# Transposing q and k by crossbar DMA instead of on TensorE, in a fused attention and feed-forward kernel

## The chip, the cores and the metric

The kernel runs on one core of one Trainium2 chip. The metric is device time in microseconds (us). Three runs of the kernel before gave a median of 439.14 us (439.12 to 439.34).

Names: PE is TensorE, PEld its weight loads, DVE is VectorE, ACT is ScalarE, POOL is GpSimd, SP is SyncE. SP issues the output stores and, after the change, the transposing DMAs; GpSimd issues the input loads. "L216" is line 216 of the kernel.

## The reference

Eight batches of eight heads, 576 tokens, head size 64, float32 inputs. Attention with a relative bias, then a feed-forward layer:

```python
scores = scale * np.matmul(q, k.transpose(0, 1, 3, 2))     # q, k, v: (8, 8, 576, 64)
scores = scores + bias.transpose(2, 0, 1)[None]            # bias_table[bucket(|i - j|)]
attn = exp(scores - max) / sum                             # softmax
x = np.matmul(attn, v)                                     # -> (4608, 512)
h = x @ w_in                                               # 512 -> 2048
out = np.maximum(0.01 * h, h) @ w_out                      # 2048 -> 512
```

## The kernel before

The kernel works on pairs of heads: 32 pairs, four to a batch. The score matmul needs q and k with the head dimension on the partitions. They are loaded with tokens on the partitions: partition `r` of 96 holds tokens `6r` to `6r+5`. So each pair's q and k are copied into a dense tile (`pr`), transposed on PE into PSUM in six blocks of 96 rows by 128 columns (the profile shows each as a matmul of 96x96), and copied out by VectorE, which also puts the tokens in order.

```python
pr_pool = ctx.enter_context(tc.tile_pool(name="pr", bufs=4))
ps_m_pool = ctx.enter_context(tc.tile_pool(name="ps_m", bufs=3, space=bass.MemoryType.PSUM))
# ... (cut)
def transpose_q(n):
    qs = prs.pop((n, "q"))
    ps = ps_m_pool.tile([P, 8 * P], BF16, name="ps_tq", tag="m")
    for c in range(NC):                                    # NC = 6, RQ = 96
        nc.tensor.transpose(ps[:, c * RQ : (c + 1) * RQ], in_=qs[0:RQ, c, :],
                            identity=ident[0:RQ, 0:RQ])
    qt = qt_pool.tile([P, S], BF16, name="qt")
    nc.vector.tensor_copy(out=qt.rearrange("p (r c) -> p r c", c=NC),
                          in_=ps[:, 0:S].rearrange("p (c r) -> p r c", c=NC))
    qts[n] = qt
# ... transpose_k is alike, and ends with two small copies inside kt
```

The main loop, one iteration per pair, interleaves everything. `moe(1)` emits one piece of feed-forward work: a group of four first-layer matmuls and its activation ("in"), or four second-layer matmuls ("out"). Pieces exist only once enough tokens have been through attention.

```python
for n in range(N + 1):
    # ... loads of later batches (cut)
    pair_rows(n + 1, "q"); pair_rows(n + 1, "k")           # VectorE: dense rows of the next pair
    ps_a, ps_b = qk_mm(n, 0), qk_mm(n, 1)                  # PE: scores; ps_s has two buffers
    exp_band(n, 0, ps_a)                                   # ScalarE: exp; VectorE: bias factor
    moe(1)
    exp_band(n, 1, ps_b)
    av(n - 1, 0)                                           # PE: attention times v; VectorE: divide
    transpose_q(n + 1)
    moe(1)
    ps_a, ps_b = qk_mm(n, 2), qk_mm(n, 3)
    exp_band(n, 2, ps_a)
    moe(1)
    exp_band(n, 3, ps_b)
    av(n - 1, 1)
    transpose_k(n + 1)
    # ... scores 4 and 5, x_transposes(n - 1), five more pieces (cut)
moe_rest()                                                 # what is left of the feed-forward layer
```

In the traces here PE, ScalarE and VectorE run their instructions in the order of the program, so an instruction that waits holds up everything behind it on its engine.

The softmax here doesn't subtract the row's maximum and nothing guards it: scores larger than these inputs give would overflow.

Of the kernel before, what the change touches and what calls it, by code (L numbers as in the profile page):

```python
# [11 lines left out]
BF16 = mybir.dt.bfloat16  # L12
# [25 lines left out]
def kernel(  # L38
# [10 lines left out]
    nc = tc.nc  # L49

    B, H, S, D = q.shape
# [4 lines left out]
    P = 128  # L56
# [12 lines left out]

    per = ctx.enter_context(tc.tile_pool(name="per", bufs=1))  # L70
    qt_pool = ctx.enter_context(tc.tile_pool(name="qt", bufs=2))
    pr_pool = ctx.enter_context(tc.tile_pool(name="pr", bufs=4))
    op_pool = ctx.enter_context(tc.tile_pool(name="op", bufs=2))
    rc_pool = ctx.enter_context(tc.tile_pool(name="rc", bufs=4))
    gt_pool = ctx.enter_context(tc.tile_pool(name="gt", bufs=2))
# [3 lines left out]
    ps_m_pool = ctx.enter_context(tc.tile_pool(name="ps_m", bufs=3, space=bass.MemoryType.PSUM))  # L79

    ident = per.tile([P, P], BF16, name="ident")
# [8 lines left out]
    NBUF = 2  # L90
    RQ = 96
    NC = S // RQ
    qn = [per.tile([P, H, NC, D], BF16, name=f"qn{i}") for i in range(NBUF)]
    kn = [per.tile([P, H, NC, D], BF16, name=f"kn{i}") for i in range(NBUF)]
    vn = [per.tile([P, NJ, H, D + 1], BF16, name=f"vn{i}") for i in range(NBUF)]
    v4 = [per.tile([P, n_pairs, 2, D + 1], BF16, name=f"v4_{i}") for i in range(NBUF)]
    kts_ = [per.tile([P, S + P], BF16, name=f"kt{i}") for i in range(2)]
# [6 lines left out]
    def load_qk(b, h0, h1):  # L104
        i = b % NBUF
        for src, dst in ((q, qn[i]), (k, kn[i])):
            nc.gpsimd.dma_start(
                out=dst[0:RQ, h0:h1, :, :].rearrange("r h c d -> r h (c d)"),
                in_=src[b, h0:h1, :, :].rearrange("h (r c) d -> r h (c d)", c=NC),
            )  # L110

    def load_v(b, h0, h1, by_head):
        i = b % NBUF
        p0, p1 = h0 // 2, h1 // 2
        if by_head:
            for h in range(h0, h1):
                nc.gpsimd.dma_start(
                    out=vn[i][:, :, h, 0:D],
                    in_=v[b, h, 0 : NJ * P, :].rearrange("(c s) d -> s c d", s=P),
                )  # L120
        else:
            for c in range(NJ):
                nc.gpsimd.dma_start(  # L123
                    out=vn[i][:, c, h0:h1, 0:D],
                    in_=v[b, h0:h1, c * P : (c + 1) * P, :].rearrange("h s d -> s h d"),
                )
        for e in range(2):
            nc.gpsimd.dma_start(
                out=v4[i][e * SL : (e + 1) * SL, p0:p1, e, 0:D],
                in_=v[b, h0 + e : h1 : 2, NJ * P : S, :].rearrange("h s d -> s h d"),  # L130
            )
# [6 lines left out]
    for i in range(2):  # L138
# [12 lines left out]
        out=tab.rearrange("p u h -> p (u h)"),  # L151
        in_=bass.AP(tensor=bias_table.tensor, offset=bias_table.offset, ap=[[0, P], [1, NB * H]]),
# [10 lines left out]
    for u, lo, hi in bucket_runs(NB, BAND, S):  # L163
        if lo >= small:
            nc.vector.tensor_copy(
                out=ub[:, :, C0 + lo : C0 + hi + 1],
                in_=e8[:, :, u : u + 1].to_broadcast([P, H, hi - lo + 1]),
# [3 lines left out]
        out=ub[:, :, C0 - BAND + 1 : C0],  # L171
        in_=bass.AP(tensor=row.tensor, offset=row.offset + C0 + BAND - 1,
                    ap=[list(row.ap[0]), [UW, H], [-1, BAND - 1]]),
# [4 lines left out]
    for h0, h1 in ((0, 2), (2, H)):  # L178
        nc.sync.dma_start(
            out=eb[:, h0:h1, :],  # L180
            in_=bass.AP(tensor=urows, offset=h0 * UW + P - 1, ap=[[H * UW - 1, P], [UW, h1 - h0], [1, 3 * P]]),
        )
    for e in range(2):
        nc.sync.dma_start(
            out=eb4[e * SL : (e + 1) * SL, :, :],
            in_=bass.AP(tensor=urows, offset=e * UW + P - 1, ap=[[H * UW - 1, SL], [2 * UW, n_pairs], [1, P + SL]]),
        )

    def load_weights():
        for c in range(n_cc):  # L190
            nc.gpsimd.dma_start(out=w_in_sb[:, c, :], in_=moe_w_in[c * P : (c + 1) * P, :])
        for g in range(n_fc // 4):
            nc.gpsimd.dma_start(
                out=w_out_sb[:, 4 * g : 4 * g + 4, :],
                in_=moe_w_out[g * 512 : (g + 1) * 512, :].rearrange("(f p) e -> p f e", p=P),
            )


    items = [(b, p) for b in range(B) for p in range(n_pairs)]
    qts, kts, ops_ = {}, {}, {}  # L200

    prs = {}

    def pair_rows(n, which):
        src = {"q": qn, "k": kn}[which]
        b, p = items[n]
        t = pr_pool.tile([RQ, NC, 2 * D], BF16, name="pr")
        nc.vector.tensor_copy(out=t.rearrange("r c (e d) -> r c e d", e=2),  # L208
                              in_=src[b % NBUF][0:RQ, 2 * p : 2 * p + 2, :, :].rearrange("r e c d -> r c e d"))
        prs[n, which] = t  # L210

    def transpose_q(n):
        qs = prs.pop((n, "q"))
        ps = ps_m_pool.tile([P, 8 * P], BF16, name="ps_tq", tag="m")
        for c in range(NC):
            nc.tensor.transpose(ps[:, c * RQ : (c + 1) * RQ], in_=qs[0:RQ, c, :],  # L216
                                identity=ident[0:RQ, 0:RQ])
        qt = qt_pool.tile([P, S], BF16, name="qt")
        nc.vector.tensor_copy(out=qt.rearrange("p (r c) -> p r c", c=NC),  # L219
                              in_=ps[:, 0:S].rearrange("p (c r) -> p r c", c=NC))  # L220
        qts[n] = qt

    def transpose_k(n):
        ks = prs.pop((n, "k"))
        ps = ps_m_pool.tile([P, 8 * P], BF16, name="ps_tk", tag="m")
        for c in range(NC):
            nc.tensor.transpose(ps[:, c * RQ : (c + 1) * RQ], in_=ks[0:RQ, c, :],  # L227
                                identity=ident[0:RQ, 0:RQ])
        kt = kts_[n % 2]
        nc.vector.tensor_copy(out=kt[:, 0:S].rearrange("p (r c) -> p r c", c=NC),  # L230
                              in_=ps[:, 0:S].rearrange("p (c r) -> p r c", c=NC))
        for e in range(2):
            r = slice(e * D, (e + 1) * D)
            nc.vector.tensor_copy(out=kt[r, S + e * SL : S + (e + 1) * SL], in_=kt[r, NJ * P : S])
        kts[n] = kt

    def qk_mm(n, u):

        qt, kt = qts[n], kts[n]
        ps = ps_s_pool.tile([P, 2, 512], FP32, name="ps_s")  # L240
        if u < NJ:
            for e in range(2):
                r = slice(e * D, (e + 1) * D)
                nc.tensor.matmul(ps[:, e, :], lhsT=kt[r, u * P : (u + 1) * P], rhs=qt[r, 0:512],  # L244
                                 start=True, stop=True)
        elif u == NJ:
            for c in range(NJ):
                for e in range(2):
                    r = slice(e * D, (e + 1) * D)
                    nc.tensor.matmul(ps[:, e, c * SL : (c + 1) * SL], lhsT=kt[r, c * P : (c + 1) * P],  # L250
                                     rhs=qt[r, 512:S], start=True, stop=True)
        else:
            nc.tensor.matmul(ps[:, 0, :], lhsT=kt[:, S : S + P], rhs=qt[:, 0:512], start=True, stop=True)  # L253
            nc.tensor.matmul(ps[:, 1, 0:SL], lhsT=kt[:, S : S + P], rhs=qt[:, 512:S], start=True, stop=True)
        return ps
# [123 lines left out]
    def finished(n):  # L379
        b, p = items[n]  # L380
        if p == n_pairs - 1:
            while made["ready"] < n_tt and (made["ready"] + 1) * TT <= (b + 1) * S:
                made["ready"] += 1

    pair_rows(0, "q")
    pair_rows(0, "k")
    transpose_q(0)
    transpose_k(0)
    N = len(items)
    for n in range(N + 1):  # L390
        live = n < N
        if live:
            b, p = items[n]
            if n == 0:
                load_qk(1, 0, H)
                load_weights()
                load_v(1, 0, H, False)
            elif p == 1 and 0 < b < B - 1:
                load_qk(b + 1, 0, H)
                load_v(b + 1, 0, H, False)  # L400
            if n + 1 < N:
                pair_rows(n + 1, "q")
                pair_rows(n + 1, "k")
            ps_a, ps_b = qk_mm(n, 0), qk_mm(n, 1)
            exp_band(n, 0, ps_a)
        moe(1)
        if live:
            exp_band(n, 1, ps_b)
        if n > 0:
            av(n - 1, 0)  # L410
        if n + 1 < N:
            transpose_q(n + 1)
        moe(1)
        if live:
# [3 lines that stand above are left out]
        if live:  # L418
            exp_band(n, 3, ps_b)
        if n > 0:  # L420
            av(n - 1, 1)
        if n + 1 < N:
            transpose_k(n + 1)
        moe(1)
        if live:
            ps_a, ps_b = qk_mm(n, 4), qk_mm(n, 5)
            exp_band(n, 4, ps_a)
        moe(1)
        if n > 0:
            x_transposes(n - 1)  # L430
            finished(n - 1)
        moe(1)
        if live:
            exp_band(n, 5, ps_b)
        moe(2)
# [31 lines left out]
```

## Time and profile before

The profile has five stages. The copies into `pr` come once per iteration, so the distance between them in the timeline is the time per pair:

| stage, us | time per pair, us | what sets it |
|---|---|---|
| 0 to 42 | - | first loads and the bias table |
| 42 to 69 | 6.1 to 6.8 | attention alone, VectorE nearly full |
| 69 to 103 | 8.5 | attention and "in" pieces |
| 103 to 364 | 11.08 | attention, "in" and "out" pieces: PE full |
| 364 to 438 | - | feed-forward alone, PE full |

The windows view of the kernel before: each row is a stretch of time, its length, the busy time and (number of) instructions of PE, PEld, DVE, ACT and POOL, then granted clock, DMA share and GB/s.

```profile
45.00:50.00 5.00, 5.00 (x77) 3.56 (x75) 4.30 (x13) 3.67 (x6) 0.57 (x2) 1.00 1.77 184
50.00:55.00 5.00, 3.79 (x62) 2.17 (x58) 4.36 (x12) 3.87 (x6) 1.29 (x2) 1.00 1.70 154
55.00:60.00 5.00, 4.06 (x81) 2.83 (x80) 4.80 (x14) 4.14 (x5) 0.00 (x0) 1.00 0.89 136
60.00:65.00 5.00, 3.86 (x71) 2.52 (x70) 4.75 (x14) 4.63 (x6) 0.63 (x1) 1.00 0.10 7
...
120.00:160.00 40.00, 40.00 (x411) 20.32 (x408) 24.73 (x63) 26.27 (x37) 6.00 (x8) 1.00 0.40 56
```

From 120 us PE is busy all the time, with VectorE at about 60% and ScalarE at about 66% (24.73 and 26.27 of 40 us). And from 45 to 55 us the DMA share is 1.7: packets overlap in time, and their times add up to 1.7 times the span of all 16 DMA engines. By their landing times (when their data has arrived) these are the last of the weight loads; the v loads of the second batch; and the q and k loads of the third batch, issued at 49.7 and 51.2 us.

What the PE transposes cost, in the timeline (start, us, engine, line, operation; "x6" is six instructions merged):

```profile
205.47 0.19 PE L303 MATMUL ps_o<-v_0_106,at_1_113 128*128 128x65 bf16 x1
205.50 0.42 PE L216 MATMUL ps_tq<-ident,pr 96*128 96x96 bf16 x6
205.75 0.60 PE L338 MATMUL pm_2911<-w_out_sb,gt 128*128 128x512 bf16 x2
```

One transpose is 206 ns long (the tile view of `ps_tq`), but they are pipelined: six of them hold up the next matmul by 0.25 us. q and k together take 0.51 us of PE per pair.

### The profile page before, as it was taken

What the parts mean: (1) busy time and instruction counts of PE and PEld (TensorE: products, weight loads), DVE (VectorE), ACT (ScalarE), POOL (GpSimd) and SP (SyncE); (2) the same over time, 40 slices, a digit from 0 to 9 for tenths busy, and PEclk for the clock granted to TensorE, in tenths of its full rate; (3) what the DMA queues carried; (4) which work ended last, traced back from release to release, by engine and by line L of the source; (5) the groups of instructions that cost most, each with busy time, mean ns of one, the idle gap of its engine ahead of it and who ended that gap; (6) DMA issues with size and microseconds to landing.
All of it is one profiled execution on the core that took longest, in us unless ns stands there. A gap on an engine that the chain in (4) does not pass through costs nothing.

```text
span 438.2 us, 9059 instructions
## 1 busy us (share of the span) xinstructions
PE 392.3 (90%) x3872; PEld 202.3 (46%) x3872; DVE 229.1 (52%) x581; ACT 247.1 (56%) x338; POOL 60.8 (14%) x84
## 2 busy tenths in 40 slices
PE   0511888999999999999999999999999999999996
PEld 0201554555555555555555555555555454444442
DVE  7331897666666666666666666666666542010111
ACT  1401787887666666666666666666666653333310
POOL 9522103103100310031003100300000000000000
PEclk9999999999999999999999999999999999999999
DMA  8999948708531853184418350900000000101111
GB/s 108 230 225 214 172 71 53 109 4 54 92 65 28 76 83 76 29 76 73 86 27 76 65 94 26 80 25 25 25 25 25 25 25 25 48 29 44 49 48 73
DMA packets 60216, 30.53 MB, mean 70 GB/s; under 512 B 39312, under 2 KB 54800, under 8 KB 60176
## 3 DMA queue, kind: packets, MB, share of 16 engines
q0 software_dynamic: 52960, 18.36, 37.6%
q1 hardware_dynamic: 7216, 11.60, 7.6%
q8 instruction: 30, 0.49, 0.5%
q14 instruction: 10, 0.08, 0.1%
HBM read 37.81 MB, written 10.49 MB: 110 GB/s over the span
## 4 chain that ended last, share of the span: by engine, by line
PE 79%; DVE 7%; DMA 7%; ACT 5%; issue 2%; SPq 0%; DVEq 0%; ACTq 0%
PE ps_o L301 7%; PE ps_s L244 6%; DMA eb_99<-u_rows 5%; PE ps_s L253 2%; DMA u_rows<-ub 2%; PE ps_o L303 2%; ACT at_110 L264 2%; ACT at_111 L264 2%; PE ps_tx L315 2%; PE ps_tq L216 1%; PE ps_tk L227 1%; PE ps_s L250 1%; DVE at_110 L288 1%; DVE opair L307 1%; ACT gt L329 1%
## 5 line engine op out<-in xcount | busy, mean ns | idle before, releaser
L264 ACT ACTIVATE at_111<-ps_s 128x1024 bf16<-128x1024 f32 x64 | 64.7, 1021 | 38.4 <-PE ps_s L244 38.3
L327 PEld LDWEIGHTS <-w_in_sb 128*128 128x128 bf16 x576 | 49.9, 98 | 72.6 <-issue 21.7
L338 PEld LDWEIGHTS <-gt 128*128 128x128 bf16 x576 | 52.6, 98 | 51.4 <-issue 0.4
L264 ACT ACTIVATE at_110<-ps_s 128x1024 bf16<-128x1024 f32 x64 | 64.3, 1021 | 20.6 <-PE ps_s L244 20.4
L288 DVE TENSOR_TENSOR at_110<-at_110,eb 128x512 bf16<-128x512 bf16 (+1 forms) x64 | 32.3, 506 | 53.0 <-ACT at_110 L264 36.8
L288 DVE TENSOR_TENSOR at_111<-at_111,eb 128x512 bf16<-128x512 bf16 (+1 forms) x64 | 32.3, 506 | 44.1 <-ACT at_111 L264 40.0
L244 PE MATMUL ps_s<-qt,kt_109 64*128 64x512 bf16 x128 | 20.8, 396 | 13.7 <-DVE kt_109 L230 13.1
L301 PEld LDWEIGHTS <-at_110 128*128 128x128 bf16 x640 | 28.3, 100 | 10.0 <-DVE opair L307 3.0
L307 DVE TENSOR_TENSOR opair<-ps_o,rcp 128x320 bf16<-128x320 f32 x64 | 31.5, 492 | 2.2
L301 PEld LDWEIGHTS <-at_111 128*128 128x128 bf16 x640 | 27.2, 98 | 9.9 <-DVE opair L307 3.0
L216 PE MATMUL ps_tq<-ident,pr 96*128 96x96 bf16 x192 | 14.2, 212 | 11.5 <-DVE pr L208 11.5
L219 DVE COPY qt<-ps_tq 128x576 bf16<-128x576 bf16 x32 | 23.9, 748 | 0.4 <-PE ps_tq L216 0.4
L244 PE MATMUL ps_s<-qt,kt_108 64*128 64x512 bf16 x128 | 21.6, 403 | 2.3 <-DVE kt_108 L230 1.2
L303 PE MATMUL ps_o<-v_0_106,at_0_112 128*128 128x65 bf16 x80 | 13.7, 200 | 8.9 <-DVE at_0_112 L288 8.8
L303 PEld LDWEIGHTS <-at_0_112 128*128 128x128 bf16 x160 | 15.9, 99 | 9.2 <-DVE at_0_112 L288 9.2
L306 DVE RECIPROCAL rcp<-ps_o 128x5 f32<-128x5 f32 x64 | 12.2, 191 | 11.4 <-PE ps_o L303 11.4
L244 PEld LDWEIGHTS <-kt_109 64*128 64x128 bf16 x128 | 4.2, 94 | 28.1 <-issue 13.8
L301 PE MATMUL ps_o<-vn_104,at_110 128*128 128x65 bf16 x320 | 15.8, 200 | 0.9 <-DVE opair L307 0.8
L123 POOL DMA_DIRECT2D vn_105<-in_v_dram x16 | 14.1, 888 | 15.5 <-PE ps_o L303 7.6
L301 PE MATMUL ps_o<-vn_104,at_111 128*128 128x65 bf16 x320 | 14.5, 194 | 1.7 <-DVE opair L307 1.7
L216 PEld LDWEIGHTS <-pr 96*128 96x128 bf16 x192 | 10.0, 101 | 12.5 <-DVE pr L208 12.4
L303 PEld LDWEIGHTS <-at_1_113 128*128 128x128 bf16 x160 | 15.6, 97 | 0.2 <-DVE at_1_113 L288 0.2
(867 smaller groups left out, 819.1 us busy)
## 6 DMA issues: line engine op xcount, KB each, us to landing
out_dram<-y SPq DMA_DIRECT2D x36, 256.0 KB, 2.0
qn_101<-in_q_dram POOLq DMA_DIRECT2D x4, 576.0 KB, 6.2
kn_103<-in_k_dram POOLq DMA_DIRECT2D x4, 576.0 KB, 8.3
w_in_sb<-in_moe_w_in_dram POOLq DMA_DIRECT2D x4, 512.0 KB, 18.5
w_out_sb<-in_moe_w_out_dram POOLq DMA_DIRECT2D x4, 512.0 KB, 23.0
vn_105<-in_v_dram POOLq DMA_DIRECT2D x16, 128.0 KB, 5.1
qn_100<-in_q_dram POOLq DMA_DIRECT2D x3, 576.0 KB, 6.0
kn_102<-in_k_dram POOLq DMA_DIRECT2D x3, 576.0 KB, 8.8
```

The costliest lines, as they stand in the source:

```text
L123: nc.gpsimd.dma_start(out=vn[i][:, c, h0:h1, 0:D], in_=v[b, h0:h1, c * P : (c + 1) * P, :].rearrange("h s d -> s h d"),)
L216: nc.tensor.transpose(ps[:, c * RQ : (c + 1) * RQ], in_=qs[0:RQ, c, :], identity=ident[0:RQ, 0:RQ])
L219: nc.vector.tensor_copy(out=qt.rearrange("p (r c) -> p r c", c=NC), in_=ps[:, 0:S].rearrange("p (c r) -> p r c", c=NC))
L244: nc.tensor.matmul(ps[:, e, :], lhsT=kt[r, u * P : (u + 1) * P], rhs=qt[r, 0:512], start=True, stop=True)
L264: nc.scalar.activation(at[:, :, u, 0:512], ps, AF.Exp, scale=scale)
L288: nc.vector.tensor_tensor(out=o, in0=o, in1=m, op=ALU.mult)
L301: nc.tensor.matmul(ps[:, ic, :], lhsT=at[:, o : o + P], rhs=vn[i][:, c, 2 * p + e, :], start=(c == 0), stop=False)
L303: nc.tensor.matmul(ps[:, ic, :], lhsT=at4[:, ic * P : (ic + 1) * P], rhs=v4[i][:, p, e, :], start=False, stop=True)
L306: nc.vector.reciprocal(rcp, ps[:, :, D : D + 1])
L307: nc.vector.tensor_tensor(out=opair[:, :, e * D : (e + 1) * D], in0=ps[:, :, 0:D], in1=rcp.to_broadcast([P, NJ + 1, D]), op=ALU.mult)
L327: nc.tensor.matmul(pm, lhsT=w_in_sb[:, c, f * P : (f + 1) * P], rhs=xT[c][:, t0 : t0 + TT], start=(c == 0), stop=(c == n_cc - 1))
L338: nc.tensor.matmul(pm, lhsT=gt[:, f, ts * P : (ts + 1) * P], rhs=w_out_sb[:, f, :], start=(f == 0), stop=(f == n_fc - 1))
```

## The change

The intent: take the transposes off PE, for all pairs but those of the first batch. One crossbar DMA per pair transposes the dense q and k rows from SBUF to SBUF; it is issued two pairs ahead. VectorE then reads SBUF, not PSUM, when it puts the tokens in order.

```diff
-    pr_pool = ctx.enter_context(tc.tile_pool(name="pr", bufs=4))
+    pr_pool = ctx.enter_context(tc.tile_pool(name="pr", bufs=3))
+    tu_pool = ctx.enter_context(tc.tile_pool(name="tu", bufs=3))
 ... (pair_rows now fills one tile [RQ, 2, NC, 2 * D] with q and k; cut)
+    def by_dma(n):
+        return items[n][0] > 0
+
+    def turn_by_dma(n):
+        t = turned[n] = tu_pool.tile([P, 2 * NC, RQ], BF16, name="tu")
+        nc.sync.dma_start_transpose(out=t, in_=prs.pop(n).rearrange("r j c d -> r (j c d)"))
+
+    def turned_pair(n, j):
+        if by_dma(n):
+            return turned[n][:, j * NC : (j + 1) * NC, :].rearrange("p c r -> p r c")
+        ps = ps_m_pool.tile([P, 8 * P], BF16, name="ps_t", tag="m")
+        ... (six PE transposes, as before; cut)
     def transpose_q(n):
-        ... (transposes on PE, cut)
-        nc.vector.tensor_copy(out=qt.rearrange("p (r c) -> p r c", c=NC),
-                              in_=ps[:, 0:S].rearrange("p (c r) -> p r c", c=NC))
+        qt = qts[n] = qt_pool.tile([P, S], BF16, name="qt")
+        nc.vector.tensor_copy(out=qt.rearrange("p (r c) -> p r c", c=NC), in_=turned_pair(n, 0))
 ... (transpose_k likewise; the q and k loads of the next batch moved from a batch's second pair to its first; cut)
-            if n + 1 < N:
-                pair_rows(n + 1, "q")
-                pair_rows(n + 1, "k")
+            if n + 1 < N and not by_dma(n + 1):
+                pair_rows(n + 1)
+            if n + 2 < N and by_dma(n + 2):
+                pair_rows(n + 2)
+                turn_by_dma(n + 2)
```

More of the change, by code (lines that the diff above doesn't have):

```diff
@@ L200, with pair_rows @@
     qts, kts, ops_ = {}, {}, {}
-    prs = {}
-    def pair_rows(n, which):
-        src = {"q": qn, "k": kn}[which]
+    prs, turned = {}, {}
+    def pair_rows(n):
         b, p = items[n]
-        t = pr_pool.tile([RQ, NC, 2 * D], BF16, name="pr")
-        nc.vector.tensor_copy(out=t.rearrange("r c (e d) -> r c e d", e=2),
-                              in_=src[b % NBUF][0:RQ, 2 * p : 2 * p + 2, :, :].rearrange("r e c d -> r c e d"))
-        prs[n, which] = t
-    def transpose_q(n):
-        qs = prs.pop((n, "q"))
-        ps = ps_m_pool.tile([P, 8 * P], BF16, name="ps_tq", tag="m")
-        for c in range(NC):
-            nc.tensor.transpose(ps[:, c * RQ : (c + 1) * RQ], in_=qs[0:RQ, c, :],
-                                identity=ident[0:RQ, 0:RQ])
-        qt = qt_pool.tile([P, S], BF16, name="qt")
-        nc.vector.tensor_copy(out=qt.rearrange("p (r c) -> p r c", c=NC),
-                              in_=ps[:, 0:S].rearrange("p (c r) -> p r c", c=NC))
-        qts[n] = qt
@@ L223, in transpose_k @@
-    def transpose_k(n):
-        ks = prs.pop((n, "k"))
-        ps = ps_m_pool.tile([P, 8 * P], BF16, name="ps_tk", tag="m")
-        for c in range(NC):
-            nc.tensor.transpose(ps[:, c * RQ : (c + 1) * RQ], in_=ks[0:RQ, c, :],
-                                identity=ident[0:RQ, 0:RQ])
-        kt = kts_[n % 2]
-        nc.vector.tensor_copy(out=kt[:, 0:S].rearrange("p (r c) -> p r c", c=NC),
-                              in_=ps[:, 0:S].rearrange("p (c r) -> p r c", c=NC))
+        t = prs[n] = pr_pool.tile([RQ, 2, NC, 2 * D], BF16, name="pr")
@@ new lines, in pair_rows @@
+        for j, src in enumerate((qn, kn)):
+            nc.vector.tensor_copy(out=t[:, j, :, :].rearrange("r c (e d) -> r c e d", e=2),
+                                  in_=src[b % NBUF][0:RQ, 2 * p : 2 * p + 2, :, :].rearrange("r e c d -> r c e d"))
+    def by_dma(n):
[7 more added lines that the diff above has]
+        ps = ps_m_pool.tile([P, 8 * P], BF16, name="ps_t", tag="m")
+        for c in range(NC):
+            nc.tensor.transpose(ps[:, c * RQ : (c + 1) * RQ], in_=prs[n][0:RQ, j, c, :],
+                                identity=ident[0:RQ, 0:RQ])
+        return ps[:, 0:S].rearrange("p (c r) -> p r c", c=NC)
@@ L232, in transpose_k @@
+    def transpose_q(n):
+        qt = qts[n] = qt_pool.tile([P, S], BF16, name="qt")
+        nc.vector.tensor_copy(out=qt.rearrange("p (r c) -> p r c", c=NC), in_=turned_pair(n, 0))
+    def transpose_k(n):
+        kt = kts[n] = kts_[n % 2]
+        nc.vector.tensor_copy(out=kt[:, 0:S].rearrange("p (r c) -> p r c", c=NC), in_=turned_pair(n, 1))
         for e in range(2):
@@ L234, in transpose_k @@
             nc.vector.tensor_copy(out=kt[r, S + e * SL : S + (e + 1) * SL], in_=kt[r, NJ * P : S])
-        kts[n] = kt
     def qk_mm(n, u):
@@ L383, in finished @@
                 made["ready"] += 1
-    pair_rows(0, "q")
-    pair_rows(0, "k")
+    pair_rows(0)
     transpose_q(0)
@@ L397 @@
                 load_v(1, 0, H, False)
+            elif p == 0 and 0 < b < B - 1:
+                load_qk(b + 1, 0, H)
             elif p == 1 and 0 < b < B - 1:
-                load_qk(b + 1, 0, H)
                 load_v(b + 1, 0, H, False)
-            if n + 1 < N:
-                pair_rows(n + 1, "q")
-                pair_rows(n + 1, "k")
+            if n + 1 < N and not by_dma(n + 1):
[3 more added lines that the diff above has]
+                turn_by_dma(n + 2)
             ps_a, ps_b = qk_mm(n, 0), qk_mm(n, 1)
```

## The prediction

> **What bounds the kernel now.** The windows view has TensorE (PE) busy 40.00 of 40 us in every stretch from 120 to 400 us, at granted clock 1.00. The waits between 110 and 340 us list none of PE matmuls. From 103 to 336 us a head pair takes 11.08 us (between copies into `pr`, timeline); VectorE is busy about 24.5 and ScalarE 27 of 40 us. Before, from 42 to 77 us, little feed-forward work is ready: a pair takes 6 to 7 us, VectorE busy 9.2 of 10 us (50:60). Pairs from 77 to 103 us take 8.5 us.
>
> **What the change removes.** For 28 of 32 pairs, two groups of six 96x96 PE transposes. One shows 206 ns, but they are pipelined: in the timeline the six for q start at 205.50 and the next matmul at 205.75, those for k at 208.89 and 209.15: 0.51 us of PE a pair. The PSUM reads by VectorE, 748 ns each, go too.
>
> **What it adds.** One 96x1536 bf16 (295 KB) crossbar DMA per pair. I estimate 1152 reads of 256 B, 72 per engine; the DMA table gives 37.6% of 16 engines' span for 52960 packets, 50 ns each, so 3.6 us, and 2 us to landing (as for output stores): 5 to 6 us. The Trainium skill, "DMA: Bandwidth & Descriptors", section "Latency and other measured facts", gives 261 GB/s for a DMA transpose: 1.1 us plus the fixed part. It is issued a period and a half before use: about 15 us of slack in the steady stage, 8 to 9 in the early one.
> VectorE's reordering copies now read SBUF. The dense 96x768 SBUF copies took 350 ns, the packed PSUM copy of 576 elements 457, the strided one 748. The Trainium skill, "VectorE: DVE Perf Modes", section "What auto-detection actually checks", has two results a cycle where source and destination are in SBUF with even outer dimensions, as here: estimate 450 ns each, 0.6 us of VectorE a pair saved.
>
> **What lies on the critical path.** Steady stage: about 22 changed pairs fall where PE never waits: about 11 us; the period becomes 10.6 us. Score matmuls come 0.25 us earlier after their exponential, which ends some 0.4 us before the second pair needs its buffer: just enough. Early stage: six changed pairs, bound by VectorE or a ScalarE/PE chain, 0.3 to 0.6 us each, 2 to 3 us. Against this: the first transposes are issued near 50 us, beside weight and q/k loads (DMA share 1.57 in 42:50, 1.29 in 50:60), and VectorE works in order, so a late one blocks everything; I allow 1 to 2 us, once.
>
> **Predicted:** 427 us, range 422 to 433; 74% faster by over 2%, 19% within 2%, 7% slower by over 2%.
>
> **What would show it.** PE matmul instructions fall by 336; steady period 10.6 us, PE still full; `qt` and `kt` copies near 450 ns (748: the SBUF read gains nothing); transposes landing 4 to 8 us after issue; no VectorE wait for `tu` after 70 us; the tail's length unchanged.
>
> **What would make it wrong.** A transpose DMA of over 10 us of throughput: DMA sets the pace, VectorE waits for `tu`, PE starves. Long waits for the first transposes. Output stores held up behind transposes in the same queue until the four `y` buffers are full. Score matmuls that begin to wait for ScalarE, eating part of the 0.5 us.

## More of the kernel before

The experiments ran in three groups on three chips, each group beside the kernel before; ratios are taken within a group.

From the page, the busy time of the engines over the whole span, and three of the rows in 40 slices of 11 us (tenths of busy time for PE and DMA; PEclk is the granted TensorE clock in tenths of full speed).

```profile
PE 392.3 (90%) x3872; PEld 202.3 (46%) x3872; DVE 229.1 (52%) x581; ACT 247.1 (56%) x338; POOL 60.8 (14%) x84
...
PE   0511888999999999999999999999999999999996
...
PEclk9999999999999999999999999999999999999999
DMA  8999948708531853184418350900000000101111
```

## The result

The changed kernel took 435.6 us (median of four runs, 435.08 to 436.23), beside 439.24 us (439.12 to 440.5) for the kernel before. The ratio is 0.991, with a 95% interval of 0.989 to 0.993. Ratios here are the mean time of one kernel's runs over the mean of the other's from the same rounds, so they are not quite the ratio of the medians quoted. It is a gain of 0.9%, where 2.8% was predicted, and outside the predicted range of 422 to 433 us.

The same lines of the page after the change:

```profile
PE 378.8 (87%) x3536; PEld 189.6 (44%) x3536; DVE 223.9 (52%) x581; ACT 246.9 (57%) x338; POOL 60.7 (14%) x84
...
PE   0520836888999999999999999999999999999996
...
PEclk9999987999999999999999999999999999999999
DMA  8999995982982597379429962952220000101111
```

The 336 PE matmuls are gone. But PE now has a hole in the sixth slice, and the granted clock falls there and in the seventh. The windows show where:

```profile
45.00:50.00 5.00, 4.83 (x74) 3.34 (x72) 4.51 (x14) 4.07 (x6) 0.68 (x1) 1.00 1.77 182
50.00:55.00 5.00, 3.86 (x71) 2.54 (x70) 4.85 (x14) 3.79 (x5) 0.98 (x2) 1.00 2.02 144
55.00:60.00 5.00, 2.68 (x49) 1.54 (x45) 2.16 (x7) 4.09 (x6) 0.00 (x0) 1.00 1.32 106
60.00:65.00 5.00, 0.00 (x0) 0.00 (x0) 0.10 (x1) 0.00 (x0) 0.00 (x0) 0.60 1.50 125
65.00:70.00 5.00, 3.30 (x36) 2.12 (x38) 4.44 (x14) 1.94 (x2) 0.00 (x0) 0.50 0.19 30
120.00:160.00 40.00, 40.00 (x407) 19.81 (x406) 25.06 (x66) 28.32 (x38) 6.35 (x8) 1.00 0.75 98
```

From 60 to 65 us the compute engines did nothing but the first 0.10 us of one VectorE copy, while the DMA share was 1.50. The chain of waits (start, us, what) names the culprit:

```profile
49.83 0.03 DVE at_113 L292
49.86 15.02 DMA tu<-pr
64.88 0.02 issue
64.90 0.64 DVE qt L232
```

The first transposing DMA took 15.0 us from issue to landing, the moment when its data had arrived. VectorE reached its copy at 57.3 us and waited 7.6 us, and as it works in order, everything waited. The tile view of `tu` has this as its only wait; the last line is the landing time in us of all 28 transposes, shortest, median and longest:

```profile
L218 SPq DMA_TRANSPOSE tu<-pr x28: 1245/1351/3547, 49.9 to 321.8; - x28
L232 DVE COPY qt<-tu x28: 640/646/654, 64.9 to 336.9; 128x576 bf16<-128x576 bf16 x28
...
  DMA tu<-pr: 7.6, 1
...
DMA to landing us min/median/max: 3.3/4.4/15.0
```

Lining up the iterations of the two kernels by the `pr` copies in the timeline (k's copy; e2_hold is an experiment told of below) shows what was won and lost where:

| start of iteration, us | before | after | e2_hold |
|---|---|---|---|
| 3 | 56.03 | 55.33 | 55.35 |
| 4 | 62.10 | 68.84 | 61.55 |
| 5 | 68.91 | 75.98 | 68.39 |
| 9 | 103.09 | 110.15 | 102.57 |
| 29 | 324.69 | 321.46 | 313.88 |
| end of span | 438.2 | 433.6 | 426.0 |

- Iterations 9 to 29: 221.60 us before, 211.31 after. That is 11.08 and 10.57 us per pair: 0.515 us gained each, as predicted (10.6).
- Iteration 3 to 4: 6.07 us before, 13.51 after, a loss of 7.4 us.
- Iteration 4 to 5: 6.81 and 7.14 us, a loss of 0.3 us. The granted clock was still 0.50 until 71.3 us; that this is the cause is not shown by this run alone (see e2_hold).
- Iterations 5 to 9: 34.18 and 34.17 us. The transposes left PE here too, and nothing was gained.

### The profile page after: what moved, and what is told of

Same layout as the page of the kernel before. It is cut to its first block, busy times and chain, and to the rows that moved or that the text cites. A ratio compares the mean times of both kernels' runs of the same rounds, so it can differ in the third digit from the quotient of the medians.

```text
span 433.6 us, 8439 instructions
## 1 busy us (share of the span) xinstructions
PE 378.8 (87%) x3536; PEld 189.6 (44%) x3536; DVE 223.9 (52%) x581; ACT 246.9 (57%) x338; POOL 60.7 (14%) x84
## 3 DMA queue, kind: packets, MB, share of 16 engines
q1 hardware_dynamic: 40368, 19.86, 25.1%
## 4 chain that ended last, share of the span: by engine, by line
PE 77%; DMA 10%; DVE 6%; ACT 4%; issue 1%; SPq 0%; DVEq 0%; ACTq 0%
PE ps_o L305 7%; PE ps_s L248 6%; DMA eb_102<-u_rows 5%; DMA tu<-pr 3%; PE ps_s L257 2%; PE ps_o L307 2%; DMA u_rows<-ub 2%; PE ps_tx L319 2%; ACT at_113 L268 1%; ACT at_114 L268 1%; PE ps_s L254 1%; ACT gt L333 1%; DVE ub L157 1%; PE pm_5412 L342 1%; DVE at_113 L292 1%
## 5 line engine op out<-in xcount | busy, mean ns | idle before, releaser
L331 PEld LDWEIGHTS <-w_in_sb 128*128 128x128 bf16 x576 | 49.9, 98 | 71.8 <-issue 20.9
L305 PEld LDWEIGHTS <-at_113 128*128 128x128 bf16 x640 | 28.3, 100 | 10.0 <-DVE opair L311 5.0
L305 PEld LDWEIGHTS <-at_114 128*128 128x128 bf16 x640 | 27.7, 99 | 10.2 <-DVE opair L311 5.2
L307 PE MATMUL ps_o<-v_0_109,at_0_115 128*128 128x65 bf16 x80 | 13.7, 200 | 10.1 <-DVE at_0_115 L292 10.0
L232 DVE COPY qt<-tu 128x576 bf16<-128x576 bf16 x28 | 18.1, 646 | 7.6 <-DMA tu<-pr 7.6
L319 PE MATMUL ps_tx<-ident,opair 128*128 128x128 bf16 x160 | 14.6, 223 | 8.0 <-DVE opair L311 8.0
L307 PEld LDWEIGHTS <-at_0_115 128*128 128x128 bf16 x160 | 15.9, 99 | 10.4 <-DVE at_0_115 L292 10.4
L129 POOL DMA_DIRECT2D v_1_110<-in_v_dram x8 | 5.1, 642 | 96.2 <-PE ps_o L307 91.4
L319 PEld LDWEIGHTS <-opair 128*128 128x128 bf16 x160 | 11.7, 100 | 15.7 <-DVE opair L311 8.9
L129 POOL DMA_DIRECT2D v_0_109<-in_v_dram x10 | 6.4, 643 | 83.7 <-PE ps_o L307 83.7
L305 PE MATMUL ps_o<-vn_107,at_113 128*128 128x65 bf16 x320 | 15.8, 200 | 0.8 <-DVE opair L311 0.8
L310 DVE RECIPROCAL rcp<-ps_o 128x5 f32<-128x5 f32 x64 | 12.2, 190 | 8.0 <-PE ps_o L307 5.1
L124 POOL DMA_DIRECT2D vn_108<-in_v_dram x16 | 14.1, 888 | 15.0 <-PE ps_o L307 7.0
## 6 DMA issues: line engine op xcount, KB each, us to landing
kn_105<-in_k_dram POOLq DMA_DIRECT2D x3, 576.0 KB, 14.1
```

Of the source, the lines that this page charges most:

```text
L124: nc.gpsimd.dma_start(out=vn[i][:, c, h0:h1, 0:D], in_=v[b, h0:h1, c * P : (c + 1) * P, :].rearrange("h s d -> s h d"),)
L305: nc.tensor.matmul(ps[:, ic, :], lhsT=at[:, o : o + P], rhs=vn[i][:, c, 2 * p + e, :], start=(c == 0), stop=False)
L307: nc.tensor.matmul(ps[:, ic, :], lhsT=at4[:, ic * P : (ic + 1) * P], rhs=v4[i][:, p, e, :], start=False, stop=True)
L310: nc.vector.reciprocal(rcp, ps[:, :, D : D + 1])
L319: nc.tensor.transpose(ps[:, ic * P : (ic + 1) * P], in_=opair[:, ic, :], identity=ident)
L331: nc.tensor.matmul(pm, lhsT=w_in_sb[:, c, f * P : (f + 1) * P], rhs=xT[c][:, t0 : t0 + TT], start=(c == 0), stop=(c == n_cc - 1))
```

## The experiments

My theory had three parts. First, the steady gain is PE time alone. Second, the first transpose lands late because the q and k loads of the third batch, issued at 49.3 and 51.4 us, hold the same DMA engines; later transposes have more slack and don't matter. Third, the pairs from 77 to 110 us are bound by a chain through ScalarE in which the PE transposes had cost nothing.

Rivals: a first transpose is slow whenever it comes; or the weight and v loads still in flight are enough to delay it; or the steady gain comes from VectorE's shorter copies or from a freer PSUM ring. All eleven runs gave correct results. The kernels of e1 to e4 were profiled twice. The figures below are of the first profile; where the second differs in a way that matters, it is said.

| run | median us (range) | ratio to before | time per pair, steady |
|---|---|---|---|
| after | 435.6 (435.08 to 436.23) | 0.991 | 10.57 |
| e1_late6 | 428.68 (427.75 to 428.9) | 0.975 | 10.57 |
| e2_hold | 427.97 (427.81 to 428.16) | 0.974 | 10.57 |
| e3_dummy | 447.05 (445.12 to 447.83) | 1.016 | 11.08 |
| e4_qonly | 434.54 (433.93 to 434.9) | 0.989 | 10.83 |
| e5_copyorder | 438.3 (437.76 to 440.28) | 0.998 | 10.57 |
| e6_ahead3 | 432.76 (432.68 to 433.26) | 0.985 | 10.57 |
| e7_reorder | 431.72 (431.12 to 432.22) | 0.982 | 10.78 |
| e8_before_reorder | 443.3 (443.03 to 443.78) | 1.009 | 11.30 |
| e9_ahead3b | 428.97 (428.21 to 431.08) | 0.977 | 10.57 |
| e10_best | 428.63 (426.57 to 429.49) | 0.974 | 10.57 |
| e11_best6 | 426.77 (426.19 to 427.21) | 0.970 | 10.57 |

The kernel before took 439.64, 439.65 and 439.51 us in the rounds of e1 to e4, e5 to e8 and e9 to e11. The 95% intervals of the ratios reach at most 0.003 to either side, so e5_copyorder can't be told from the kernel before.

### e1_late6: the first transposes come later

```diff
     def by_dma(n):
-        return items[n][0] > 0
+        return n >= 6
```

> Pairs 4 and 5 go back to PE; the first transpose is issued some 12 us later, when the q and k loads of the third batch are nearly through. Theory (the first transposes wait for DMA engines that the weight and q/k loads fill): first landing 5 to 9 us, VectorE wait for tu under 1 us, no PE gap near 60 us, clock 1.00 throughout, 428 to 429.5 us (ratio 0.975 to 0.978). Rival (a first transpose is slow whenever it comes): first landing still near 15 us, VectorE waits 4 us or more, 433 us or more. In both the steady period stays 10.57 us.

It took 428.68 us. The first transpose was issued at 61.9 us and landed in 3.5 us, sooner than the 5 to 9 us expected:

```profile
tu<-pr SPq DMA_TRANSPOSE x1, 3.5
```

No VectorE copy waited for `tu`, and the lowest granted clock in the 10 us windows from 40 to 100 us was 1.00. A first transpose is therefore not slow as such. Two pairs fewer by DMA made the kernel about 6.9 us faster (428.68 against 435.6).

### e2_hold: the loads come later

```diff
             elif p == 0 and 0 < b < B - 1:
+                if b == 1:
+                    nc.gpsimd.tensor_copy(out=held, in_=qts[n][:, 0:1])
                 load_qk(b + 1, 0, H)
... (held is one small tile in SBUF; cut)
```

GpSimd's small copy makes it wait for qt of pair 4, and its two loads with it.

> The changed kernel as it is, but GpSimd may start the third batch's q/k loads only when qt of pair 4 is written. Theory A (those two loads are what the first transpose waits behind): first landing 5 to 8 us, VectorE wait for tu of pair 4 under 1 us; the loads now meet the transposes of pairs 5 to 7, so up to 2 us of waits there; 428 to 431 us. Theory B (weights and v of the second batch, issued earlier, are enough): first landing 10 us or more, wait 3 to 7 us, 432 to 436 us.

It took 427.97 us. The first transpose was issued at the same time as in the changed kernel (49.9 us), beside the same earlier loads. The DMA issues in the window from 49 us, first of the changed kernel (with the two loads beside it), then of e2_hold (landing time in us at the end):

```profile
qn_103<-in_q_dram POOLq DMA_DIRECT2D x1, 576.0 KB, 9.6
kn_105<-in_k_dram POOLq DMA_DIRECT2D x1, 576.0 KB, 14.1
tu<-pr SPq DMA_TRANSPOSE x1, 15.0
```

```profile
tu<-pr SPq DMA_TRANSPOSE x1, 5.1
```

So 10 of the 15 us were due to those two loads, and theory A holds (in the second profile of e2_hold the first landing was 4.0 us). The earlier loads beside it were the v loads of the second batch rather than weights: in e2_hold all but 3 of the 2404 packets between 49 and 51 us are under 512 B, and the weights move in packets of 1024 B.

```profile
DMA packets 2404, 0.31 MB, mean 153 GB/s; under 512 B 2401, under 2 KB 2404, under 8 KB 2404
```

The transpose that met the held loads took 9.1 us, and nothing waited for it. The next one, issued at 68.7 us beside the q and k loads of the fourth batch, took 12.3 us, and VectorE's only wait for `tu` was for that one (idle time before it in brackets):

```profile
81.10 0.65 DVE L234 COPY qt<-tu 128x576 bf16<-128x576 bf16 x1 [0.28 <-DMA tu<-pr]
```

In the first profile the granted clock fell here too, to 0.73 from 60 to 65 us, although PE was busy for 4.35 of these 5 us; in the second it did not. Iterations 4 to 9 took 41.02 us in the first and 40.77 in the second. This fits a loss of some 0.3 us by the clock, here and in the changed kernel, but why the clock fell stays open.

### e3_dummy: the PE work put back

```diff
         if by_dma(n):
+            idle = ps_m_pool.tile([P, 8 * P], BF16, name="ps_idle", tag="m")
+            for c in range(NC):
+                nc.tensor.transpose(idle[:, c * RQ : (c + 1) * RQ], in_=eb[0:RQ, 0, c * 32 : c * 32 + P],
+                                    identity=ident[0:RQ, 0:RQ])
             return turned[n][:, j * NC : (j + 1) * NC, :].rearrange("p c r -> p r c")
```

> The changed kernel with twelve idle 96x96 PE transposes per pair put back where the old ones stood, their result unused (VectorE does not read it). If the steady gain is PE time alone: period 11.08 us again, 446 to 448 us (ratio 1.015 to 1.02). If the gain comes from VectorE's shorter copies or the PSUM ring: period stays below 10.8 us and the time near 436 us.

It took 447.05 us, with 11.08 us per pair: the pace of the kernel before, although VectorE had the shorter copies (a line of the tile view, with the shortest, median and longest copy in ns, and a row of the windows view):

```profile
L236 DVE COPY qt<-tu x28: 636/642/655, 65.1 to 347.9; 128x576 bf16<-128x576 bf16 x28
120.00:160.00 40.00, 40.00 (x414) 20.20 (x412) 23.67 (x60) 26.64 (x36) 6.35 (x8) 1.00 0.65 86
```

The steady gain is PE time alone. The idle transposes also take a PSUM buffer each time, so e3 does not part PE time from the PSUM ring; but between 110 and 340 us the waits of the kernel before list none of a PE matmul, so PE did not wait for a buffer there. The 7.4 us wait for the first transpose was still there (6.4 us in the second profile), so this kernel has the loss without the gain.

### e4_qonly: half the bytes

```diff
-        t = turned[n] = tu_pool.tile([P, 2 * NC, RQ], BF16, name="tu")
-        nc.sync.dma_start_transpose(out=t, in_=prs.pop(n).rearrange("r j c d -> r (j c d)"))
+        t = turned[n] = tu_pool.tile([P, NC, RQ], BF16, name="tu")
+        nc.sync.dma_start_transpose(out=t, in_=prs[n][:, 0, :, :].rearrange("r c d -> r (c d)"))
...
-        if by_dma(n):
+        if by_dma(n) and j == 0:
```

> Only q goes by DMA (half the bytes), k stays on PE. If PE time alone sets the steady pace: period 10.83 us, 5.4 us of steady gain in place of 10.8. First landing, if the engines are shared in proportion to packets: 8 to 12 us in place of 15, VectorE wait 1 to 4 us; total 435 to 437.5 us. If the wait does not depend on the transpose's size: wait still 7 us and 440 us.

It took 434.54 us, a little under the range. The steady pair took 10.83 us: half the PE work removed, half the gain. The window from 49 us:

```profile
qn<-in_q_dram POOLq DMA_DIRECT2D x1, 576.0 KB, 8.1
kn<-in_k_dram POOLq DMA_DIRECT2D x1, 576.0 KB, 10.5
tu<-pr SPq DMA_TRANSPOSE x1, 7.7
```

Half the bytes landed in half the time (7.7 us in place of 15.0), beside the same loads, and the loads landed sooner too. This fits DMA engines that the queues share by packets, but the sharing is not shown to be even: in the changed kernel's profile the queue of the loads and that of the transposes moved 328 and 348 packets between 58 and 62 us, but 217 and 605 between 56 and 58. The transpose, issued at 50.1 us, landed just before VectorE reached its copy at 57.9 us, so VectorE didn't wait at all, where I had expected 1 to 4 us after a landing of 8 to 12.

### e5_copyorder: the reordering copies the other way round

```diff
-        ...tensor_copy(out=qt.rearrange("p (r c) -> p r c", c=NC), in_=turned_pair(n, 0))
+        ...tensor_copy(out=qt.rearrange("p (r c) -> p c r", c=NC), in_=turned_pair(n, 0).rearrange("p r c -> p c r"))
```

The copy for kt likewise, on top of e1_late6; it also holds for the copies from PSUM of the first six pairs.

> On top of e1_late6 the two VectorE copies into token order walk the other way: they read runs of 96 adjacent elements and write with a step of six. If VectorE gives two results a cycle for any pattern that is in SBUF on both sides, and the 646 ns come from reading with a step of 96, the copies fall to 440 to 480 ns; the time falls by 0 to 1.5 us against e1_late6 (only the stage before 75 us has these copies on its chain). If the step costs the same on the write side, they stay at 620 to 660 ns and the time does not move.

Neither expectation held. The by-form groups of this run (busy us in all, mean ns of one):

```profile
L232 DVE COPY qt<-tu 128x576 bf16<-128x576 bf16 x26 | 29.7, 1142 | 0.8 <-DMA tu<-pr 0.8
...
L232 DVE COPY qt<-ps_t 128x576 bf16<-128x576 bf16 x6 | 12.5, 2080 | 0.4 <-PE ps_t L226 0.4
```

Writing with a step of six elements costs much more than reading with a step of 96: 1142 ns in place of 646 from SBUF, 2080 in place of 750 from PSUM. The time, 438.3 us, shows where VectorE counts. The steady pairs still took 10.57 us, but those before 77 us took 8.4 to 8.6 us in place of 6.1 to 6.6. Each of these has two copies from PSUM, 2.7 us more work for VectorE, which is busy for 9.72 of the 10 us from 50 to 60. So the stage of attention alone is bound by VectorE in this run, and the copies are on its path.

### e6_ahead3 and e9_ahead3b: more lead time, the loads left where they were

```diff
-            if n + 2 < N and by_dma(n + 2):
-                pair_rows(n + 2)
-                turn_by_dma(n + 2)
+            if n + 3 < N and by_dma(n + 3):
+                pair_rows(n + 3)
+                turn_by_dma(n + 3)
```

> The changed kernel, with every transpose issued three pairs ahead in place of two, so the first goes out near 43 us and is needed near 57 us. Theory (lead time short against a landing stretched by the weight and q/k loads): first landing 10 to 15 us, VectorE wait for tu 0 to 2 us, 428 to 430.5 us, although the DMA traffic is the same. Rival (transposes and loads cost each other engine time that must be paid whatever the lead): wait of 4 us or more somewhere before 80 us, 432 us or more.

It took 432.76 us, outside the theory's range and inside the rival's. No copy waited for `tu`, but VectorE waited 3.1 us to overwrite a `pr` tile:

```profile
DVE pr L210 <- DMA tu<-pr: 3.1, 1, 3.1
```

The ring of three `pr` tiles was full: the first transpose, issued at 43.6 us, had not read its rows until 53.1. I had moved the wait from the transpose's output to its input. e9_ahead3b is the same with `bufs=4` for `pr`.

> e6_ahead3 with a fourth buffer for the rows that a transpose reads. In e6 no copy waited for tu, but VectorE waited 3.1 us to overwrite rows that the first transpose had not yet read (issued 43.6, read until 53.1). Theory (that ring of three was the whole of e6's loss): no wait for tu or pr over 0.5 us, PE clock 1.00, 427.5 to 429.5 us, with the loads left where they were. Rival (early transposes slow the weight or q/k loads, and something else waits for those): a wait of 2 us or more elsewhere, 431 us or more.

It took 428.97 us, and VectorE waited for neither `tu` nor `pr`, although the transposes issued at 50.2, 56.4 and 62.3 us took 13.5, 10.7 and 10.3 us to land. The DMA traffic was not the loss; the lack of lead time was.

### e7_reorder and e8_before_reorder: the chain in the pairs of 8.48 us

The chain of waits of the kernel before, in one such pair:

```profile
87.57 1.03 ACT at_111 L264
88.59 0.04 issue
88.64 0.39 PE ps_s L244 x2
89.03 0.98 PE pm_1143 L327 x4
90.01 0.02 issue
90.03 0.60 ACT gt L329
```

And after the change:

```profile
94.63 1.03 ACT at_114 L268
95.66 0.04 issue
95.70 0.39 PE ps_s L248 x2
96.09 0.98 PE pm_1089 L331 x4
97.08 0.02 issue
97.10 0.60 ACT gt L333
```

It is the same chain: an exponential frees a score buffer, the score matmul fills it, the "in" piece stands behind it in PE's order, its activation waits for it, and the next exponential stands behind that. The q transposes stood just before that score matmul, where PE had to wait anyway. In the timeline PE's wait there was 0.27 us before the change and 0.53 us after: the time was freed and turned into waiting.

The reordering lets PE do the "in" piece first:

```diff
-            ps_a, ps_b = qk_mm(n, 2), qk_mm(n, 3)
+            ps_a = qk_mm(n, 2)
             exp_band(n, 2, ps_a)
         moe(1)
         if live:
+            ps_b = qk_mm(n, 3)
             exp_band(n, 3, ps_b)
... (scores 4 and 5 likewise)
```

e7_reorder has it on top of e1_late6, e8_before_reorder on the kernel before.

> On top of e1_late6 PE does the next feed-forward group before the second score matmul of a step, which must wait for ScalarE's exponential to free its buffer. Theory (the 8.48 us pairs between 76 and 102 us are bound by a chain ScalarE - score matmul - feed-forward matmuls - ScalarE, in which the PE transposes sat in a wait of PE): those pairs fall to 7.3 to 7.8 us, the steady period stays 10.57 us, the time falls by 2.5 to 5 us against e1_late6, to 423.5 to 426 us. Rival (something else holds these pairs): 8.3 us or more and 428 us or more.

> The same reordering on the kernel before. Without that chain these pairs are bound by PE, which is busy 7.85 of 8.48 us there with the transposes and 7.35 without. So I expect them at 7.8 to 8.2 us, 0.3 to 0.5 us longer than in e7_reorder: there the transposes' PE time does count. Steady period 11.08 us; total 437 to 438.5 us. If the pairs come out equal in the two kernels, PE is not what bounds them then either.

The pairs of 8.48 us fell to 7.85 us in e7 (a little above my range) and to 8.11 us in e8 (inside it). The last pair before the steady stage did not gain: 8.57 us before, 8.71 in e7 and 8.82 in e8. The windows of one such pair, e7 first and then e8:

```profile
84.57:92.42 7.85, 7.39 (x91) 3.90 (x89) 5.77 (x17) 7.08 (x11) 0.00 (x0) 1.00 0.21 40
```

```profile
84.46:92.57 8.11, 7.91 (x105) 4.38 (x101) 5.91 (x18) 7.08 (x11) 0.00 (x0) 1.00 0.11 18
```

With the chain broken, the PE work shows: 7.91 us of PE in 8.11 with the transposes, 7.39 in 7.85 without. In the pairs of 8.48 us the same two amounts of PE work (7.89 before, 7.38 after) had taken equally long. Half of the freed 0.52 us (0.26 us) now shortens the pair. So the third part of the theory holds.

But both kernels became slower in all (431.72 us against 428.68 for e1_late6, and 443.3 against 439.65), outside both ranges, which I had not expected: the steady pair took 0.21 us more in e7 (10.78 against 10.57) and 0.22 us more in e8 (11.30 against 11.08). In e7's timeline the score matmuls of a step, four in a row elsewhere, are split in two groups of two around the "in" piece. The timeline shows what the split costs: two score matmuls hold up the next one for 0.32 us each time, 0.64 in all, where four in a row take 0.54; and the "in" piece between them takes 0.97 us, not 0.87. That is 0.20 of the 0.21 us. Why is not shown.

### e10_best and e11_best6: the reordering only where the chain is

The reordering is applied in iterations 5 to 8 alone, on e2_hold (e10) and on e1_late6 (e11).

```diff
-            ps_a, ps_b = qk_mm(n, 2), qk_mm(n, 3)
+            ps_a = qk_mm(n, 2)
+            if not 5 <= n <= 8:
+                ps_b = qk_mm(n, 3)
             exp_band(n, 2, ps_a)
         moe(1)
         if live:
+            if 5 <= n <= 8:
+                ps_b = qk_mm(n, 3)
             exp_band(n, 3, ps_b)
... (scores 4 and 5 likewise; cut)
```

> e2_hold with the reordering of e7 in iterations 5 to 8 alone. Expected: those four pairs at 7.85 us in place of 8.48, steady period 10.57 us, as in e2; 425 to 426 us.

> e1_late6 with the reordering of e7 in iterations 5 to 8 alone: the same four pairs at 7.85 us, steady period 10.57 us; 425.5 to 426.8 us.

e11_best6 took 426.77 us, 3.0% less than the kernel before and the lowest median of all. Three of the four pairs took 7.85 to 7.91 us; the fourth took 8.70 and did not gain. The steady pair took 10.57. e10_best missed its range: 428.63 us, with a spread of 2.9 us. In its profile VectorE waited 2.5 us for a transpose issued at 69.2 us, which took 13.9 us beside the q and k loads of the fourth batch (issued at 69.3 and 70.1 us). In e2_hold the transpose of the same pair took 12.3 us and made VectorE wait for 0.3; here the pairs had become shorter, and with them the lead that is counted in pairs.

## Why the prediction was wrong

The prediction was 427 us; the measured time was 435.6. Point by point:

- **Steady stage: right.** "About 11 us; the period becomes 10.6 us", with PE still full. Measured: 0.515 us a pair, 10.57 us, so 22 x 0.515 = 11.3 us. e3, e4 and the waits show that this is PE time and nothing else. ScalarE did not get in the way. The tail was unchanged as predicted: 74.0 us from the last attention matmul to the end before, 73.7 after.
- **First transposes: the step that failed.** "A late one blocks everything; I allow 1 to 2 us, once." The mechanism was named, the size was wrong: 7.4 us, and 0.3 us more while the clock was low. The term that failed is the landing time: I had estimated 5 to 6 us to landing and 8 to 9 us of slack, and it was 15.0 us beside the loads, with a slack of 7.5 us (49.86 to 57.33). That the median of all 28 (4.4 us) lies near the estimate is luck: a quiet transpose moved its 1152 packets within 1.65 us, not 3.6, and landed in 3.3, and those beside a batch's loads took up to 12.2 us in the steady stage. The prediction itself quotes a DMA share of 1.57 and 1.29 at that time, and I did not carry it into the landing time. The Trainium skill, "DMA: Bandwidth & Descriptors", section "Issuing engines are not separate DMA queues", says that DMAs from all issuing engines run on the same 16 DMA engines and interleave. This agrees: 15.0 us with both loads, 5.1 without them (e2), 7.7 with half the bytes (e4); and the k load, 8.8 us in the kernel before, took 14.1 beside the transposes.
- **Early gain: wrong.** "Six changed pairs, 0.3 to 0.6 us each, 2 to 3 us." Measured without the stall, in e2_hold: iterations 4 to 9 took 41.02 us (40.77 in the second profile), against 40.99 before. In the pairs of 8.48 us the freed PE time fell into a wait of PE (e7, e8). In the stage bound by VectorE the copies were 0.1 us shorter each and not 0.3.
- **Copies: wrong.** "Near 450 ns." Measured 646, where the copy from PSUM took 748.
- **No VectorE wait for `tu` after 70 us: right,** and the output stores were not held up: their median landing stayed 2.0 us.

Together: a stall some 6 us larger than allowed and an early gain some 2.5 us smaller account for the 8.6 us between 427 and 435.6. With the stall taken away (e2_hold) the kernel stands at 428.0, inside the predicted range: the stall alone put it outside. That this is so near 427 is partly luck, as the early gain of 2 to 3 us, which did not come, and the 1 to 2 us allowed for the stall nearly cancel in the forecast.

## What to carry to other kernels

Moving work from a full engine to DMA gains what the engine's pipelined pace says, here 0.51 us of PE a pair, but only in the stage where that engine sets the pace; look for the chain in each stage before counting. The transfer must be issued earlier by its landing time under the loads that run beside it, not by its quiet landing time: here that was 15 us in place of 3.3, and one late transfer ahead of an in-order engine cost two thirds of the gain. Where the first few transfers fall into a time of heavy loading, leave those few on the old path, hold back loads that have time, or issue further ahead with enough buffers on both sides; all three gave 428 to 429 us.

## What the Trainium skill lacked or had wrong

- "VectorE: DVE Perf Modes", section "What auto-detection actually checks": two results a cycle where source and destination of a one-source op are in SBUF with even outermost dimensions. The copy of 128x576 bf16 that reads 96 runs of six elements with a step of 96 took 646 ns, where I had estimated 450 from that rule. The runs do not show why. The skill has no figure for a stepped write of 2-byte elements (its measured stepped streams, in "Vector Engine (DVE) Microarchitecture Reference", are of 4-byte elements): the same copy with a step of six on the write side took 1142 ns from SBUF and 2080 ns from PSUM.
- "TensorE: Matmul & The Clock Gate", section "Part 4: PE-mode transpose": about 275 ns in a kernel's context for 128x128, and no pace for several in a row. The profile shows 206 ns for one transpose of 96 rows, but six of them held up the next matmul by only 0.25 us, 42 ns each. A cost per transpose taken from the single duration would have been five times too high.
- "DMA: Bandwidth & Descriptors", section "Latency and other measured facts", gives a bandwidth for DMA transposes, 261 GB/s measured on one kernel, but no landing time from SBUF to SBUF, nor how far other traffic stretches it. Here one of 96x1536 bf16 (295 KB, 1184 packets: 40368 less 7216 on the hardware queue, over 28) moved its data within 1.65 us when quiet, about 180 GB/s (the one issued at 321.8 us), and landed in 3.3 us at best, 4.4 us in the median and 15.0 us beside two loads of 576 KB.
